# Efficient attention and mixture of depths: ranks as accumulated VectorE columns, a 0/1 matmul for the search, one unit's transposes and product in one slot

## The chip, the core and the metric

One core of a Trainium2 chip runs the whole problem. The metric is device microseconds of one execution, as the median of several. Five engines with instruction streams of their own take part: TensorE (PE in the rows; its weight loads are PEld), VectorE (DVE), ScalarE (ACT), GpSimd (POOL) and SyncE (SP, which here only issues DMAs). Each works its own instructions off in the order in which they were written and waits on semaphores for the others.

## What is computed

```python
def _attn_ref(q, k, v):                       # (8, 8, 576, 64) each
    q_s = softmax(q, axis=-1); k_s = softmax(k, axis=2)
    kv = np.einsum('bhsd,bhse->bhde', k_s, v)
    return np.einsum('bhsd,bhde->bhse', q_s, kv)

def _moe_ref(x, w_gate, w1, w2, capacity):    # x (8, 576, 512), capacity 128
    scores = np.einsum('bsd,d->bs', x, w_gate)
    out = x.copy()
    for b in range(B):
        top_idx = np.argpartition(-scores[b], capacity)[:capacity]
        xe = x[b, top_idx]
        ye = np.maximum(xe @ w1, 0.0) @ w2
        g = 1.0 / (1.0 + np.exp(-scores[b, top_idx]))
        out[b, top_idx] = x[b, top_idx] + g[:, None] * ye
```

The attention's heads are laid side by side and become x. Per batch the 128 tokens of highest score go through an MLP of 512 x 1024 x 512 and are written back over their rows.

## The kernel before

A **unit** is four heads of one batch: 16 units, two to a batch. Its 576 tokens lie on 128 partitions in five columns r (R = 5), the last half filled. For a unit u, `k_exp` and `q_exp` take exponentials on ScalarE, `v_copy` lays v beside a column of ones on VectorE, `kv_mm` multiplies K and V into 64 x 65 blocks (40 matmul instructions in the trace, since each fp32 matmul stands there twice), and `kv_out` inverts the sums (`krec`) and copies the blocks into a block-diagonal `kv_diag` that also holds a column for the score. `q_t(u, i)` transposes four columns of one half of the heads on TensorE, and ScalarE evacuates them into `qT`; `q_t_last` does the fifth column of both halves, evacuated by VectorE. `x_mm(u, i)` multiplies qT with kv_diag, and `x_out(u, i)` divides by q's sums into `xs` on VectorE and takes the scores into `sr`; the rows of the output then go out from the SP queue.

Of a batch's scores, `score` sums the head shares, `score_row` lays them as a row on all partitions (five transposes on TensorE, evacuated by ScalarE), `compare` makes on VectorE the 0/1 planes `less` and `ties` of every token against every other, `count` adds them over the partitions with 16 matmuls against ones (`ones_b`) and gives the ranks as a row, and `pick` finds for each of the 128 places the token whose rank it is (two passes of 640 columns that sum a product), computes the gate g and has POOL gather the rows from the output in DRAM (`xr`). `turn` transposes the gathered rows, `mlp1` and `mlp2` are the two halves of the MLP in eight pieces each, and `finish` adds and scatters.

The order is written by hand. The loop over slots s = 0 .. 19 works on unit s, prepares units s + 1 and s + 2, and lays MLP pieces between: batch b has its scores ready in slot 2b + 1, is compared in 2b + 2, counted and picked in 2b + 3 behind the fourth MLP piece, and its MLP runs in slots 2b + 4 (`turn` and `mlp1`) and 2b + 5 (`mlp2`). In slot s, TensorE has kv_mm(s + 1) and q_t(s + 1, 0) ahead of x_mm(s, 0); k_exp, v_copy and q_exp of unit s + 2 follow the products. A slot with mlp1 is called even below, one with mlp2 odd. PSUM holds two banks `tp` (transposes, K-V, counts), two pairs `x` and two banks `mm`. Loads of q, k and v go round three buffers, two DMAs each, all from SP's queue: load(s + 5) in slot s.

Of the kernel before, what the change touches and what calls it, by code (L numbers as in the profile page):

```python
# [8 lines left out]
F32 = mybir.dt.float32  # L9
# [8 lines left out]
def kernel(  # L18
# [20 lines left out]
    nc = tc.nc  # L39
# [5 lines left out]
    RP = R * P  # L45
# [6 lines left out]
    NG = 4 * R  # L52
    LOW = 2.0 ** -30
    WARM = 20
    assert S == 64 * (R + N2) and D == 64 and DM == H * D and DM == 512 and H % 4 == 0
    assert 1 < capacity < S and KF == 8 and NQ == 2
    HALF = RP // 2
# [27 lines left out]
    def load(u, which):  # L85
        b, qd = units[u]
        for what in which:
# [3 lines left out]
            for n, rows in enumerate((R, N2)):  # L91
                nc.sync.dma_start(
# [7 lines left out]
    load(0, "kvq")  # L100
# [12 lines left out]
    for n in range(20):  # L113
        nc.tensor.matmul(out=w_ps[part(n % 2), :132], lhsT=ones_f[:, :64], rhs=ones_f, start=True, stop=True)
# [33 lines left out]
    for h in range(2):  # L148
        nc.vector.memset(side[part(h), h:h + 1], 1.0)
    qrec = const.tile([P, NU, NG], F32, name="qrec")  # L150
    krec = const.tile([P, NU, 2], F32, name="krec")

    col_minus_p = const.tile([P, P], F32, name="col_minus_p")
    nc.gpsimd.iota(col_minus_p, pattern=[[1, P]], base=0, channel_multiplier=-1,
                   allow_small_or_imprecise_dtypes=True)
    after = const.tile([P, P], F32, name="after")
    tok_row = const.tile([P, RP], F32, name="tok_row")
    nc.gpsimd.iota(tok_row.rearrange("p (r m n) -> p r m n", r=R, n=2), pattern=[[1, R], [9, 64], [R, 2]], base=0,  # L158
                   channel_multiplier=0, allow_small_or_imprecise_dtypes=True)
    slot_no = const.tile([P, n_sl], F32, name="slot_no")  # L160
    for n, (k0, _) in enumerate(slots):
        nc.gpsimd.iota(slot_no[:, n:n + 1], pattern=[[1, 1]], base=k0, channel_multiplier=1,
                       allow_small_or_imprecise_dtypes=True)

    def late_constants():
        nc.vector.tensor_scalar(after, col_minus_p, 0.0, None, op0=OP.is_gt)
# [59 lines left out]
    def q_t_last(u):  # L226
        qe = st.pop(("qe", u))
# [7 lines left out]
    def x_mm(u, i):  # L235

        qT = st["qT", u] if i == 0 else st.pop(("qT", u))
        x_ps = ps.tile([P, 2, 512], F32, tag="x", name="x", bufs=2)
        x = x_ps[:, :, :6 * C].rearrange("p n (g h c) -> p n g h c", g=3, h=2)
        for r in range(R):  # L240
            nc.tensor.matmul(out=x[:, r // 3, r % 3], lhsT=qT[:, i, r], rhs=kv_diag[u % 2][:, i],  # L241
                             start=True, stop=True)
        st["x", u] = x
# [3 lines left out]
    def x_out(u, i):  # L247
        b, qd = units[u]
        if qd == 0 and i == 0:
            xs[b] = xp.tile([P, R, NQ, 2, 2, D], F32, tag="xs", name="xs")  # L250
            sr[b] = md.tile([P, NQ, 2, R, 2], F32, tag="sr", name="sr")
        x = st.pop(("x", u))
        rec = qrec[:, u].rearrange("p (i r h) -> p i r h", i=2, r=R)[:, i]
# [338 lines left out]
```

## Time and profile before

| | |
|---|---|
| time, median of 3 runs | 294.73 us (293.66 to 295.18) |
| profiled execution, its own time | 297.34 us |
| its span, first to last instruction | 295.5 us |
| mean granted TensorE clock | 0.920 |
| busy share PE, PEld, DVE, ACT, POOL | 80%, 65%, 49%, 34%, 7% |
| instructions | 5206 |
| DMA | 46.69 MB, 158 GB/s in the mean |

A busy TensorE is not TensorE at full clock: 1.00 of granted clock is 2.4 GHz, and the other level is 1.2. A stretch in which it waits and one in which it runs at the lower level both have to be looked for in the rows. The engines off the chain that sets the end may idle for nothing.

### The profile page before, as it was taken

How to read it: one execution, taken by the hardware profiler on the slowest of the kernel's cores; microseconds unless marked ns; L12 is line 12 of the kernel's file. 1: busy time of each engine (PE TensorE's matmuls, PEld its weight loads, DVE VectorE, ACT ScalarE, POOL GpSimd, SP SyncE). 2: the span in 40 equal slices, each digit the busy share in tenths (PEclk: the TensorE clock that was granted, in tenths of full speed). 3: DMA queues.
4: the chain of work that ended last, by engine and by line, in shares of the span. 5: the costliest groups of instructions: out<-in, count | busy, mean ns of one | idle time of the engine just before them, and what ended most of it. 6: DMA issues, size and time to landing. Idle time of an engine off the chain costs nothing.

```text
span 295.5 us, 5206 instructions
## 1 busy us (share of the span) xinstructions
PE 237.3 (80%) x2021; PEld 191.7 (65%) x2021; DVE 143.9 (49%) x506; ACT 99.1 (34%) x178; POOL 22.1 (7%) x32
## 2 busy tenths in 40 slices
PE   6468748229997699949996799969996999799990
PEld 6368638129963698529963798549963995484840
DVE  7454495503864176613863167615753386640001
ACT  3574444303352154315351153425351311130100
POOL 8000000100001100020001100020001000210101
PEclk9997796957999799998999599989999899999997
DMA  6999999880589218551649119220221122101101
GB/s 194 359 357 367 383 382 382 251 291 2 165 295 284 111 63 258 167 191 38 198 153 296 66 40 284 81 68 5 80 81 38 38 80 80 58 15 38 38 7 39
DMA packets 39329, 46.69 MB, mean 158 GB/s; under 512 B 2945, under 2 KB 36737, under 8 KB 39297
## 3 DMA queue, kind: packets, MB, share of 16 engines
q1 hardware_dynamic: 37472, 41.95, 43.4%
q0 software_dynamic: 1280, 4.20, 4.1%
q8 instruction: 18, 0.29, 0.4%
q10 hardware_dynamic: 544, 0.13, 0.2%
q14 instruction: 15, 0.11, 0.1%
HBM read 34.73 MB, written 11.53 MB: 157 GB/s over the span
## 4 chain that ended last, share of the span: by engine, by line
PE 65%; DMA 18%; issue 7%; DVE 3%; POOL 2%; ACT 2%; SPq 1%; POOLq 0%; ACTq 0%
PE mm L360 20%; PE mm L370 15%; DMA xr<-out_dram,idx 11%; PE x L241 10%; PE tp L194 8%; PE tp L221 4%; PE tp L312 4%; DMA q<-in_q_dram 3%; PE mm L346 2%; DMA out_dram<-xs 2%; DMA k<-in_k_dram 2%; DVE junk_p L325 2%; POOL tok_row L158 1%; ACT rank L314 1%; PE tp L230 1%
## 5 line engine op out<-in xcount | busy, mean ns | idle before, releaser
L360 PE MATMUL mm<-xT,w 128*128 128x128 f32 x512 | 65.2, 284 | 1.4 <-ACT xT L348 1.4
L360 PEld LDWEIGHTS mm<-xT,w 128*128 128x128 f32 x512 | 61.8, 199 | 2.5 <-ACT xT L348 1.9
L370 PE MATMUL mm<-w,hT 128*128 128x512 f32 x128 | 61.4, 600 | 0.0
L241 PE MATMUL x<-kv_diag,qT 128*128 128x132 f32 x320 | 43.3, 285 | 0.0
L241 PEld LDWEIGHTS x<-kv_diag,qT 128*128 128x128 f32 x320 | 41.3, 200 | 2.4 <-issue 2.4
L194 PE MATMUL tp<-v_ones,ke 128*64 128x65 f32 x640 | 29.6, 265 | 8.0 <-DVE v_ones L184 4.3
L194 PEld LDWEIGHTS tp<-v_ones,ke 128*64 128x64 f32 x640 | 27.1, 177 | 11.3 <-ACT qe L180 4.8
L257 DVE TENSOR_TENSOR xs<-x,qrec 128x384 f32<-128x384 f32 x64 | 31.4, 491 | 2.2
L370 PEld LDWEIGHTS mm<-w,hT 128*128 128x128 f32 x128 | 21.7, 191 | 14.9 <-issue 14.3
L223 ACT ACTIVATE qT<-tp,krec 128x512 f32<-128x512 f32 x32 | 22.0, 687 | 27.1 <-PE tp L221 27.0
L346 PE MATMUL mm<-ident,xr 128*128 128x128 f32 x32 | 7.2, 367 | 27.2 <-DMA xr<-out_dram,idx 27.2
L203 DVE RECIPROCAL krec<-tp 128x2 f32<-128x2 f32 x16 | 2.7, 170 | 48.7 <-PE tp L194 48.7
L256 DVE RECIPROCAL qrec<-x 128x6 f32<-128x6 f32 x64 | 11.8, 184 | 29.8 <-PE x L241 29.5
L346 PEld LDWEIGHTS mm<-ident,xr 128*128 128x128 f32 x32 | 4.7, 180 | 32.9 <-DMA xr<-out_dram,idx 32.4
L221 PE MATMUL tp<-ident,qe 128*128 128x128 f32 x128 | 21.6, 296 | 4.5 <-DVE krec L203 3.1
L330 POOL DMA_INDIRECT xr<-out_dram,idx x8 | 7.9, 988 | 219.9 <-PE tp L281 105.4
L180 ACT ACTIVATE qe<-q 128x640 f32<-128x640 f32 x32 | 21.7, 726 | 3.6 <-DMA q<-in_q_dram 3.6
L363 ACT ACTIVATE hT<-mm 128x512 f32<-128x512 f32 x16 | 9.6, 597 | 37.8 <-PE mm L360 37.8
L221 PEld LDWEIGHTS tp<-ident,qe 128*128 128x128 f32 x128 | 16.7, 154 | 7.9 <-issue 4.9
L173 ACT ACTIVATE ke<-k 128x1280 f32<-128x1280 f32 x16 | 20.2, 1261 | 2.8 <-DMA k<-in_k_dram 2.8
L378 DVE SCALAR_TENSOR_TENSOR o<-mm,g,xr 128x512 f32<-128x512 f32 x8 | 6.0, 749 | 27.1 <-PE mm L370 27.1
L348 ACT COPY xT<-mm 128x512 f32<-128x512 f32 x8 | 4.7, 586 | 42.2 <-PE mm L346 42.2
(71 smaller groups left out, 220.3 us busy)
## 6 DMA issues: line engine op xcount, KB each, us to landing
k<-in_k_dram SPq DMA_DIRECT2D x16, 320.0 KB, 5.0
v<-in_v_dram SPq DMA_DIRECT2D x16, 320.0 KB, 5.2
q<-in_q_dram SPq DMA_DIRECT2D x16, 320.0 KB, 5.7
out_dram<-xs SPq DMA_DIRECT2D x16, 320.0 KB, 2.8
k<-in_k_dram SPq DMA_DIRECT2D x16, 256.0 KB, 4.9
v<-in_v_dram SPq DMA_DIRECT2D x16, 256.0 KB, 5.5
q<-in_q_dram SPq DMA_DIRECT2D x16, 256.0 KB, 6.2
out_dram<-xs SPq DMA_DIRECT2D x16, 256.0 KB, 3.0
```

The source lines that it names most:

```text
L173: nc.scalar.activation(out=ke, in_=raw["k"][u % LD], func=AF.Exp)
L180: nc.scalar.activation(out=qe[:, i], in_=qr[:, i], func=AF.Exp)
L194: nc.tensor.matmul(out=kv[part(h), i], lhsT=ke[:, 2 * i + h, r], rhs=vo[:, 2 * i + h, r], start=(r == 0), stop=(r == N2))
L221: nc.tensor.transpose(out=t_ps[:, r * P:(r + 1) * P], in_=qe[:, i, r].rearrange("p h d -> p (h d)"), identity=ident)
L223: nc.scalar.activation(out=st["qT", u][:, i, :N2].rearrange("p r c -> p (r c)"), in_=t_ps, func=AF.Copy, scale=krec[:, u, i:i + 1])
L241: nc.tensor.matmul(out=x[:, r // 3, r % 3], lhsT=qT[:, i, r], rhs=kv_diag[u % 2][:, i], start=True, stop=True)
L256: nc.vector.reciprocal(out=rec[:, rows], in_=o[:, :, :, D])
L257: nc.vector.tensor_mul(xs[b][:, rows, qd, i], o[:, :, :, :D], rec[:, rows].to_broadcast([P, rows.stop - rows.start, 2, D]))
L312: nc.tensor.matmul(out=r_ps[:, a:z], lhsT=ones_b[:, :P], rhs=rhs, start=(n == 0), stop=(n == len(todo) - 1), skip_group_check=True)
L346: nc.tensor.transpose(out=t_ps[:, d * m:(d + 1) * m], in_=xr[:m, d * P:(d + 1) * P], identity=ident[:m, :m])
L360: nc.tensor.matmul(out=h_ps[:, f % 4 * m:(f % 4 + 1) * m], lhsT=w1[:, d, f * P:(f + 1) * P], rhs=xT[:, d, :m], start=(d == 0), stop=(d == ...
L370: nc.tensor.matmul(out=st["y", b, n][:m], lhsT=st["hT", b, n][:, f, :m], rhs=w2[:, f], start=(f == 0), stop=(f == KF - 1))
```

## The change

*Ranks.* Instead of 0/1 planes counted by matmuls, `compare(b, r)` is one VectorE pass over 576 columns (score row minus own score, against a threshold of a tiny number or zero that orders equal scores) with an accumulator that leaves the rank of each token in column r. *Search.* `pick` compares ranks with the place numbers into a 0/1 tile `hit` (one VectorE instruction of 640 columns) and multiplies it with `vals`, which holds token number and score split into five bf16 columns; five matmuls of 5 columns give both at once. POOL makes the score's three parts in `score`, five small operations per batch. The gate's exponential has moved into `gate`, later in the slot. *Products.* `x_out` has one reciprocal and one narrow product for both groups. *Order.* A unit's transposes now stand at the head of its own slot and its product behind them; kv_mm(s + 1) follows its own slot's first product; `v_copy(s + 1)`, `k_exp(s + 1)` and `q_exp(s + 1)` stand in slot s. `pick` stands near the slot's head. *Loads.* load(s + 4) in slot s, w1 and w2 earlier, unit 0's k from two queues. *Constants.* `late_constants` holds five 576-wide passes and a dozen small operations. The program's check of its ranges has six values instead of four.

```diff
     def late_constants():
-        nc.vector.tensor_scalar(after, col_minus_p, 0.0, None, op0=OP.is_gt)
+        nc.vector.tensor_single_scalar(odd_p, odd_p, 1, op=OP.bitwise_and)
...
+        nc.vector.tensor_copy(out=vals[:, :, :, 0], in_=whole.rearrange("p (b r) -> p b r", b=B))
...
+        for r in range(R):
+            nc.vector.tensor_scalar(not_before[:, r], order_minus_p, float(r * P), TINY, op0=OP.is_ge, op1=OP.mult)
...
+        nc.vector.reciprocal(out=rec, in_=x[:, :, :, D])
         for n, rows in enumerate((slice(0, 3), slice(3, R))):
...
-            nc.vector.reciprocal(out=rec[:, rows], in_=o[:, :, :, D])
...
-            nc.vector.tensor_mul(sr[b][:, qd, i, rows], o[:, :, :, D + 1], rec[:, rows])
...
-    def compare(b):
-        s, srow = st["s", b], st["srow", b]
...
-    def count(b):
...
+    def compare(b, r):
...
+        nc.vector.scalar_tensor_tensor(junk, st["srow", b], st["s", b][:, r:r + 1], not_before[:, r],
+                                       op0=OP.subtract, op1=OP.is_ge, accum_out=st["rank", b][:, r:r + 1])
...
+            nc.vector.tensor_tensor(out=hit[:, :, :m], in0=slot_no[:, None, k0:k0 + m].to_broadcast([P, R, m]),
+                                    in1=rank.to_broadcast([P, R, m]), op=OP.is_equal)
+            c_ps = bank("tp", 2)
             for r in range(R):
...
+                nc.tensor.matmul(out=c_ps[:m, :NV], lhsT=hit[:, r, :m], rhs=vals[:, b, r],
+                                 start=(r == 0), stop=(r == N2))
...
+            if here:
+                q_t(s, 0)
+                q_t_last(s)
             if first:
                 each(turn, mlp_b)
-            if s + 1 < NU:
+            else:
+                pieces(1)
+            if here:
+                q_t(s, 1)
+            if chosen is not None:
+                pick(chosen)
+            if not first:
+                pieces(1)
+            if here:
+                x_mm(s, 0)
+                x_out(s, 0)
+            if after:
+                k_exp(s + 1)
+                v_copy(s + 1)
+            pieces(2 if first else 1)
+            if last:
+                x_mm(s, 1)
+                x_out(s, 1)
+                x_store(s)
+                score(ends)
+            if after:
                 kv_mm(s + 1)
                 kv_out(s + 1)
...
+            if compared is not None:
+                for r in range(2):
+                    compare(compared, r)
+            pieces(1)
+            if here and not last:
                 x_mm(s, 1)
                 x_out(s, 1)
...
+                x_store(s)
             if last:
                 score_row(ends)
-                compare(ends)
+                for r in range(R):
+                    compare(ends, r)
+            if chosen is not None:
+                each(gate, chosen)
+            if ends is not None and not last:
+                score(ends)
+            if after:
+                q_exp(s + 1)
...
+            if compared is not None:
+                for r in range(2, R):
+                    compare(compared, r)
             pieces(2)
```

TensorE in slot 4, the first with an MLP, before: L346 turns the gathered rows, L194 is K-V, L360 mlp1 (four matmuls a piece), L221 and L230 are q's transposes, L241 its product.

```order
L346 MATMUL mm<-ident,xr 128x128 x4
L194 MATMUL tp<-v_ones_183,ke 64x65 x20
L360 MATMUL mm<-xT,w_162 128x128 x4
L221 MATMUL tp<-ident,qe 128x128 x4
L241 MATMUL x<-kv_diag_181,qT 128x132 x5
L221 MATMUL tp<-ident,qe 128x128 x4
L360 MATMUL mm<-xT,w_162 128x128 x4
L241 MATMUL x<-kv_diag_181,qT 128x132 x5
L360 MATMUL mm<-xT,w_162 128x128 x4
L230 MATMUL tp<-ident,qe 128x128 x2
L360 MATMUL mm<-xT,w_162 128x128 x20
```

The same slot now; L397 turns the gathered rows, L260 and L269 are q's transposes, L280 the product, L411 mlp1, L233 K-V:

```order
L260 MATMUL tp<-ident,qe 128x128 x4
L269 MATMUL tp<-ident,qe 128x128 x2
L397 MATMUL mm<-ident,xr 128x128 x4
L260 MATMUL tp<-ident,qe 128x128 x4
L280 MATMUL x_189<-kv_diag_178,qT 128x132 x5
L411 MATMUL mm<-xT,w_159 128x128 x8
L233 MATMUL tp<-v_ones_180,ke 64x65 x20
L411 MATMUL mm<-xT,w_159 128x128 x4
L280 MATMUL x_191<-kv_diag_178,qT 128x132 x5
L411 MATMUL mm<-xT,w_159 128x128 x20
```

K-V has gone from the slot's head to behind the first product and two pieces, and the transposes, now the unit's own, to the head.

VectorE in slot 5, before, where the first MLP's batch is in mlp2 and batch 1 is searched: L184 lays v beside the ones, L232 evacuates the last transposes, L325 is the search.

```order
L184 COPY v_ones_183<-v_84 128x20x64
L232 TENSOR_TENSOR qT<-tp,krec 128x2x128
L325 SCALAR_TENSOR_TENSOR junk_p,sel<-rank,slot_no,tok_row 128x640
L325 SCALAR_TENSOR_TENSOR junk_p,sel<-rank,slot_no,srow 128x640
L328 TENSOR_SCALAR idx<-sel 128x1
L335 TENSOR_SCALAR g<-g 128x1
L336 RECIPROCAL g<-g 128x1
```

The same slot now, from its head; L364 to L374 are the search, L292 to L298 x_out, L223 v_copy:

```order
L271 TENSOR_TENSOR qT<-tp,krec 128x2x128
L364 TENSOR_TENSOR hit<-slot_no,rank 128x640
L372 TENSOR_REDUCE no<-tp 128x1
L373 TENSOR_SCALAR idx<-no 128x1
L374 TENSOR_REDUCE no<-tp 128x1
L292 RECIPROCAL qrec<-x_189 128x12
L295 TENSOR_TENSOR xs<-x_189,qrec 128x3x128
L295 TENSOR_TENSOR xs<-x_189,qrec 128x2x128
L298 TENSOR_TENSOR sr<-x_189,qrec 128x12
L223 COPY v_ones_175<-v_82 128x20x64
```

v's copy stands now behind the search and the first x_out of the slot that uses it, and before behind the products of the slot ahead of that.

VectorE from v_copy(0) on at the start, before; L203 to L211 are kv_out, L232 evacuates unit 0's last transposes, L184 is the copy of v:

```order
L184 COPY v_ones_178<-v_82 128x20x64
L166 TENSOR_SCALAR after<-col_minus_p 128x128
L203 RECIPROCAL krec<-tp 128x2
L208 TENSOR_TENSOR prod<-tp,wg 128x128
L210 TENSOR_REDUCE kvw<-prod 128x2
L211 TENSOR_TENSOR kv_diag_181<-kvw,side 128x4
L232 TENSOR_TENSOR qT<-tp,krec 128x2x128
L184 COPY v_ones_183<-v_83 128x20x64
```

Now, from inside the constants, which follow kv_out(0), to the same point:

```order
L202 COPY valid_r<-beyond 128x1
L203 TENSOR_SCALAR valid_r<-valid 128x1
L205 TENSOR_SCALAR not_before<-order_minus_p 128x576 x5
L271 TENSOR_TENSOR qT<-tp,krec 128x2x128
L292 RECIPROCAL qrec<-x_189 128x12
L295 TENSOR_TENSOR xs<-x_189,qrec 128x3x128
L295 TENSOR_TENSOR xs<-x_189,qrec 128x2x128
L298 TENSOR_TENSOR sr<-x_189,qrec 128x12
L223 COPY v_ones_180<-v_83 128x20x64
```

Before, one small constant stands ahead of kv_out(0); now the constants stand between kv_out(0) and the evacuation of the transposes.

## Rows read from the trace of the kernel before

**Rows 1.** Table of stretches: bounds, length, busy us (and instructions) PE, PEld, DVE, ACT, POOL, clock, DMA share, GB/s

```profile
15.09:22.70 7.61, 4.95 (x71) 4.61 (x71) 4.58 (x18) 5.61 (x9) 0.00 (x0) 1.00 1.08 357
...
40.94:64.60 23.66, 9.73 (x91) 8.63 (x92) 11.62 (x42) 5.90 (x12) 1.13 (x1) 0.76 0.98 335
64.60:98.31 33.71, 29.50 (x246) 23.89 (x246) 17.07 (x60) 12.21 (x22) 0.95 (x1) 0.91 0.58 185
...
131.11:164.22 33.11, 28.35 (x245) 22.91 (x245) 17.07 (x60) 12.21 (x22) 1.97 (x2) 0.93 0.50 160
...
227.76:254.83 27.07, 25.61 (x195) 20.32 (x196) 16.97 (x64) 5.38 (x12) 1.96 (x2) 0.94 0.19 64
254.83:273.05 18.22, 16.99 (x103) 12.28 (x104) 5.13 (x19) 2.83 (x6) 1.96 (x2) 1.00 0.10 31
273.05:295.50 22.45, 14.71 (x84) 10.30 (x82) 1.50 (x2) 1.78 (x3) 1.97 (x2) 0.93 0.08 27
```

**Rows 2.** List of waits: who waited for whom: us in total, times, longest

```profile
PE mm L346 <- DMA xr<-out_dram,idx: 27.2, 7, 8.7
```

**Rows 3.** Chain that ended last, one pair of slots: start us, us, what

```profile
131.77 2.18 PE tp L194 x40
133.95 1.79 PE mm L360 x8
...
137.74 0.89 PE mm L360 x8
...
145.33 1.32 PE tp L194 x40
...
147.71 0.44 PE tp L221 x4
148.14 1.13 PE x L241 x10
...
152.77 0.86 PE mm L370 x2
153.63 0.83 PE tp L312 x8
...
154.96 0.98 PE tp L312 x8
...
159.09 5.09 DMA xr<-out_dram,idx
```

**Rows 4.** TensorE in order of time near 164 and 255: start, us, what, [idle before, releaser]

```profile
164.22 1.11 PE L346 MATMUL mm<-ident,xr 128*128 128x128 f32 x4 [4.24 <-DMA xr<-out_dram,idx]
...
254.83 0.66 PE L346 MATMUL mm<-ident,xr 128*128 128x128 f32 x4 [1.39 <-DMA xr<-out_dram,idx]
...
256.16 3.84 PE L360 MATMUL mm<-xT,w 128*128 128x128 f32 x32 [0.68 <-ACT xT L348]
```

**Rows 5.** Groups by line and shape: line, engine, operation, names, shapes, count | busy us, mean ns | idle before

```profile
L223 ACT ACTIVATE qT<-tp,krec 128x512 f32<-128x512 f32 x32 | 22.0, 687 | 27.1 <-PE tp L221 27.0
...
L180 ACT ACTIVATE qe<-q 128x640 f32<-128x640 f32 x32 | 21.7, 726 | 3.6 <-DMA q<-in_q_dram 3.6
...
L257 DVE TENSOR_TENSOR xs<-x,qrec 128x384 f32<-128x384 f32 x32 | 17.8, 558 | 1.1
...
L257 DVE TENSOR_TENSOR xs<-x,qrec 128x256 f32<-128x256 f32 x32 | 13.6, 425 | 1.1
L184 DVE COPY v_ones<-v 128x1280 f32<-128x1280 f32 x16 | 13.1, 820 | 1.9 <-DMA v<-in_v_dram 1.9
...
L206 ACT COPY kv_diag<-tp 64x130 f32<-64x130 f32 x32 | 8.4, 262 | 26.9 <-DVE krec L203 26.5
...
L325 DVE SCALAR_TENSOR_TENSOR junk_p<-rank,slot_no,tok_row 128x640 bf16<-128x640 f32 x8 | 7.1, 885 | 18.3 <-ACT rank L314 18.3
...
L256 DVE RECIPROCAL qrec<-x 128x6 f32<-128x6 f32 x32 | 6.3, 196 | 29.8 <-PE x L241 29.5
...
L292 DVE TENSOR_SCALAR less<-srow,s 128x640 bf16<-128x640 f32 x8 | 4.4, 546 | 0.0
```

More of the change, by code (lines that the diff above doesn't have):

```diff
@@ L112 @@
     w_ps = bank("tp", 2)
-    for n in range(20):
-        nc.tensor.matmul(out=w_ps[part(n % 2), :132], lhsT=ones_f[:, :64], rhs=ones_f, start=True, stop=True)
+    w_ps2 = bank("tp", 2)
+    for n in range(24):
+        a, c = ((0, 0), (1, 1), (0, 1), (1, 0))[n % 4 if n >= 12 else n % 2]
+        nc.tensor.matmul(out=(w_ps, w_ps2)[a][part(c), :66], lhsT=ones_f[part(a), :64],
+                         rhs=ones_f[part(a), :66], start=True, stop=True)
     for n in range(WARM):
@@ L158 @@
[L158 to L163, printed above, removed]
[L165 to L166 removed]
+    x_buf = []
@@ L273, in score @@
         st["s", b] = s
+        left = md.tile([P, R], F32, tag="left", name="left")
+        for c in range(2, NV):
+            nc.gpsimd.tensor_copy(out=vals[:, b, :, c], in_=raw_s if c == 2 else left)
+            if c < NV - 1:
+                nc.gpsimd.tensor_sub(left, raw_s if c == 2 else left, vals[:, b, :, c])
     def score_row(b):
@@ L431, in general @@
                     x_out(u, i)
-            score(b)
+                x_store(u)
+            score(b, 0)
             score_row(b)
-            compare(b)
-            count(b)
+            for r in range(R):
+                compare_exact(b, r)
             pick(b)
+            each(gate, b)
             each(turn, b)
@@ L459, in sums_in_range @@
         return number
-    def prepare(u):
-        k_exp(u)
-        v_copy(u)
-        q_exp(u)
     LAG = 4
@@ L503, in pieces @@
                     f_next += 1
-            ends = s // 2 if s % 2 == 1 and s < NU else None
-            compared = (s - 2) // 2 if s % 2 == 0 and 2 <= s < NU else None
+            here = s < NU
+            after = s + 1 < NU
+            last = s == NU - 1
+            ends = s // 2 if here and s % 2 == 1 else None
+            compared = s // 2 - 1 if s % 2 == 0 and 2 <= s < NU else None
             chosen = (s - 3) // 2 if s % 2 == 1 and 3 <= s < NU else None
@@ L514 @@
+            if after:
[8 more added lines that the diff above has]
+            if after:
                 kv_mm(s + 1)
                 kv_out(s + 1)
-                pieces(1)
-                q_t(s + 1, 0)
-            elif not last:
-                pieces(1)
-            if s < NU:
-                x_mm(s, 0)
-                x_out(s, 0)
@@ L535 @@
[L535 to L549 removed]
+                x_store(s)
             if last:
                 score_row(ends)
[L552 removed]
+                for r in range(R):
+                    compare(ends, r)
@@ L553 @@
             pieces(2)
-            if last:
-                pieces(1)
-            pieces(1)
             if ends is not None and not last:
                 score_row(ends)
-            pieces(1)
+            pieces(3 if first else 2)
             if busy and odd == 1:
```

247 lines of the change are left out of this document (130 added, 117 removed).

## Prediction, made before the changed kernel was run

> **What bounds the kernel now.** I read the table of stretches first [rows 1]. Cut at the transposes of the gathered rows (L346), which open the MLP of a batch, the program falls into a start (to 64.60 us), five pairs of slots (163.2 us to 227.76), two last stretches and a tail. In a pair such as 131.11 to 164.22 TensorE is busy for 28.35 of 33.11 us, VectorE for 17.07, ScalarE for 12.21, and DMA for half: TensorE bounds, and it is neither full nor at full clock (0.93). Where it loses time the chain shows [rows 3]. The gather runs 5.09 us from 159.09, and the transposes that start at 164.22 have 4.24 us of nothing ahead of them [rows 4]. After such a gap TensorE runs at the lower level: the 40 K-V matmuls take 2.18 us against 1.32 later in the pair, and the first eight MLP matmuls 1.79 against 0.89, so another 1.76 us. The list of waits says the same in sum: 27.2 us of TensorE's waiting for gathered rows, seven times, at most 8.7 [rows 2].
>
> What a pair costs at full clock comes from the pieces in [rows 3]: K-V 2 x 1.32, transposes of q 2 x (0.44 + 0.44 + 0.22), products 4 x 1.13, first MLP half 8 x 0.89, second 8 x 0.86, turning xr 0.44, score rows 0.55 (five transposes): 24.3 us. Gap 4.2, slow clock 1.8 and the count (153.63 to 155.94) 2.3 make 32.6 of the 33.1.
>
> **The change, part by part.** *The count leaves TensorE.* 16 ones-matmuls with their evacuations go: 2.3 us a pair [rows 3]. In their place are five 0/1 matmuls of 5 columns, whose like no row shows. Between nothing (they slip in beside weight loads) and 0.8 (half the count they replace) I take 0.3.
>
> *The gather is issued a slot earlier.* The search now stands near the head of slot 2b+3, and the MLP opens in 2b+4 as before. From search to opening lie some 11 us of slot against a gather of 5.09: the gap and the slow clock behind it go, 6.0 us a pair.
>
> *VectorE.* The nine compares and five tie products of a batch become five 576-wide passes with an accumulator. A 640-wide one takes 0.89 [rows 5]; 576 columns with the reading of the accumulator I put at 0.88, so 4.4 in all; the two 640-wide searches become one 640-wide compare. From 0.56 at 384 and 0.43 at 256 columns that is 0.82. VectorE's sum falls and stays far from TensorE's; its order matters more.
>
> *What comes late next.* One unit's work is now in one line in one slot. kv_mm(s+1) stands behind v_copy(s+1), which stands on VectorE behind x_out(s,0), which waits for x_mm(s,0). Before, v_copy was done a slot ahead. x_out is a reciprocal, two products and a narrow product (priced as the reciprocal): 0.20 + 0.56 + 0.43 + 0.20 = 1.4; v_copy 0.82 [rows 5]; with 0.15 of hand-over 2.35 us. Between x_mm(s,0) and kv_mm(s+1) TensorE has two MLP pieces in the even slot (1.78), one in the odd (0.86). It stalls 0.6 and 1.5 us. Two smaller ones: in the even slot the second transposes need the first's PSUM bank, evacuated in 0.69 [rows 5] beside 0.66 of other work, 0.2 with hand-over; in the odd slot score_row waits for x_out(s,1) and three small score operations with two pieces (1.72) as cover, 0.4. Three of the compares end the even slot; VectorE then has the last q product (as before) and the 0/1 compare ahead of it. By durations that ends within 0.1 us of where TensorE asks for it, so nothing is taken, 0.8 if the cover is short.
>
> So a pair: 24.3 + 0.3 + 0.8 + 1.9 = **27.3 us**. If none of the stalls showed it would be 24.6; if each were 0.8 longer than worked out in both slots, 28.9. The first pair I give 1 us of slow clock. From the first opening to the sixth: before 64.60 to 227.76, 163.2 [rows 1]; after 5 x 27.3 + 1 = 137.5. **-25.7.**
>
> *The start.* The wait of 8.7 for the first gather goes, but the four slots without an MLP have no filler any more. In line a slot is: transposes 0.44, evacuation 0.8, second transposes 0.44, product 1.13, x_out 1.4, v_copy 0.82, K-V 1.32, reciprocal and two copies 0.8, first exp of q 0.73 [rows 3, 5]: 7.9 us, 0.3 of hand-over, and 3.3 us of it on a TensorE at 0.76 as in [rows 1] (+1.0): 9.2. Before, kv_mm(1) to kv_mm(4) is 15.09 to 40.94, 8.6 a slot. Ahead of kv_mm(1) now stand the new constants (five 576-wide passes of at most 0.55 and a dozen small ones of at most 0.20 [rows 5], 5.1 us at most; 4.2 taken, since they overlap at their ends; all on VectorE in front of slot 0's q product) and that slot's product in line, 2 us: 21.3. Three slots bring 27.6, the score row of slot 1 with its wait 2.4, five compares and the 0/1 compare ahead of slot 3's q product 5.2: kv_mm(4) at 56.5. To the first opening come 1.3 + 1.13 + 1.4 + 0.6 + 0.55 + 0.7 + 0.66 and 1 of clock: 7.3, so 63.8 against 64.6. **-0.8**, between -6 (constants and half the compares beside DMA waits) and +5 (half clock throughout). The loads cover this: each is issued three slots ahead as before. The weights move up the SP queue, w1 to just behind unit 3 and w2 behind units 5 and 6; at the 335 GB/s of [rows 1], unit 5 is there by about 45 and is wanted after 60. x_store now stands on SP ahead of the next loads, as before.
>
> *The end.* From the sixth opening to the eighth, before 227.76 to 273.05, 45.3 [rows 1]. After: rest of slot 14 12.2, slot 15 11.1 of work and 1.0 for the last score row. In slot 16 five compares, the gate and finish stand on VectorE ahead of the last 0/1 compare, and the search is ahead of the MLP pieces on TensorE: after score_row come its evacuation 0.9, the compares 4.4, gate and finish 1.1, the 0/1 compare 0.82, 7.3 with hand-over, covered by four second-half pieces and the turn of xr, 3.9: a stall of 3.4. With 0.44 + 0.3 + 7.1 that is 11.2, slot 17 6.9, slow clock after the stall 1.0: 43.4. **-1.9** (0 to -4). The last 22.45 us keep their chain, 0.
>
> Sum: -0.8 - 25.7 - 1.9 = -28.4. The profiled execution took 297.34 us around a span of 295.5 and would take 268.9; it lay 2.6 above the median of 294.73, and against that the forecast is **266.3 us**.
>
> **Rivals.** *The clock does not stay up.* The new stalls come twice a slot. If one in each of the 11 slots that prepare another unit costs what the gaps of [rows 3] cost, 1.76 us, the time is 266.3 + 19.4 = 286. Against it: at 254.83 TensorE had just been idle 1.39 us and was idle another 0.68 before its 32 MLP matmuls, which took 3.84 us against 3.6 elsewhere, and that stretch has a granted clock of 1.00 [rows 1, 4]. For it: the longest new stall, 1.5, is longer than any of these. The Trainium skill, "TensorE: Matmul & The Clock Gate", section "A second HAM failure mode: psum-queue depth-cycling", speaks against the change here: frequent small idles between groups of matmuls make the clock fall and recover over and over. By that rule this rival's 286 would hold; the 1.00 of [rows 1] does not bear it out at 1.39 us. Chance 14%.
>
> *The stalls are covered and the start is short.* VectorE takes the next instruction a little before the one ahead is out, so x_out and v_copy may take 0.4 less; with pairs of 25.6 (-8.5) and a start of 60 (-4) the time is 254. Chance 16%.
>
> *Slower.* One place: the MLP slots run at the clock of the slots before them, 0.76 [rows 1], because transposes, product and copies of one unit hang in one line there too. A pair is then 24.6 / 0.76 + 2.7 = 35.1; five are +39 and slots 14 and 15 +8 on the forecast, 313 us. It decides against the change from a clock under 24.6 / (32.6 - 2.7) = 0.82 on. Against it: half of TensorE's work in these slots is MLP, which waits for nothing in the line. Chance 4%.
>
> *The gather is not what holds the opening*, and the pair keeps its 33 us because the evacuation of the gathered rows or VectorE's finish comes last. Against it: in [rows 2] the opening waits for the gather and nothing else. Time 294. Chance 1%.
>
> **How the numbers follow.** Forecast 65%, clock 14%, better cover 16%, slower 4%, no effect 1%. The forecast's own bounds are 266.3 - 10 and + 12 (start ±5, five pairs +8 or -8, end ±2, not all at once). The range of 254 to 281 leaves out the clock rival's upper half, the slower case and the lower tail of the better one, about 2 in 10. Faster by over 0.5% (what a measurement of this kernel can tell from no change): 0.94; within 0.5%: 0.02; slower: 0.04.
>
> **What would show it.** Right: no wait of TensorE for gathered rows; pairs of about 27 us with a granted clock over 0.97; waits of kv_mm for v_copy near 1.5 and 0.6 us; the first opening near 64; one stall of some 3 us in slot 16 for the 0/1 compare. Wrong: K-V matmuls of 2 us and more inside the pairs (clock), openings before 60 or after 69 (the start), a 576-wide pass well off 0.88, or a wait of TensorE for the 0/1 compare in each odd slot.

## The result and the profile after

| | before | changed kernel |
|---|---|---|
| time, median | 294.96 us (293.66 to 299.37, 4 runs) | 278.71 us (276.59 to 279.93, 4 runs) |
| ratio | | 0.946 (95% interval 0.938 to 0.953) |
| profiled execution, span | 295.5 us | 277.0 us |
| first opening (turn of xr) | 64.60 | 70.24 |
| first to sixth opening, five pairs | 163.16 | 139.61 |
| sixth to eighth opening | 45.3 | 44.64 |
| behind the eighth | 22.45 | 22.51 |

The forecast was 266.3 us in a range of 254 to 281. The kernel became faster, less than forecast: the pairs gave 23.6 of the 25.7 us that they were to give, and the start grew by 5.6 us where it was to shrink by 0.8.

The table of stretches of the changed kernel answers to [rows 1]: bounds in us, length, then busy us and instructions of PE, PEld, DVE, ACT and POOL, granted clock, DMA share, GB/s.

```profile
0.00:22.07 22.07, 10.91 (x121) 9.72 (x121) 10.23 (x48) 7.17 (x10) 3.37 (x18) 1.00 0.90 285
22.07:30.43 8.36, 5.44 (x70) 4.73 (x71) 4.29 (x14) 4.42 (x7) 0.00 (x0) 1.00 0.98 324
30.43:45.49 15.06, 9.88 (x76) 8.68 (x76) 5.00 (x17) 5.12 (x9) 0.98 (x5) 0.63 1.02 340
45.49:60.80 15.31, 9.47 (x76) 8.55 (x76) 9.36 (x28) 4.42 (x7) 1.17 (x1) 0.61 0.63 203
60.80:70.24 9.44, 6.71 (x61) 6.18 (x62) 2.77 (x13) 2.68 (x7) 0.98 (x5) 0.68 0.72 234
70.24:98.54 28.30, 26.28 (x236) 20.86 (x236) 15.02 (x48) 11.31 (x20) 2.01 (x6) 0.97 0.57 181
...
126.36:154.19 27.83, 25.63 (x236) 20.25 (x235) 15.22 (x49) 11.22 (x20) 3.01 (x7) 1.00 0.60 188
...
209.85:234.94 25.09, 23.35 (x190) 18.39 (x189) 15.50 (x48) 8.19 (x15) 2.97 (x7) 1.00 0.21 70
234.94:254.49 19.55, 16.76 (x92) 12.51 (x90) 6.48 (x27) 1.98 (x4) 2.33 (x2) 0.91 0.08 28
```

Two things stand out. A pair has gone from 33.11 to 27.83 us at a granted clock of 1.00 instead of 0.93. And three stretches of the start run at 0.61 to 0.68, lower than the 0.76 of before: more of the time at the 1.2 GHz level, where 1.00 is 2.4 GHz throughout.

The list of TensorE's waits (who for whom: us in total, times, longest) answers to [rows 2]:

```profile
PE tp L233 <- DVE v_ones L223: 17.3, 15, 2.2
PE tp L331 <- DVE s L316: 7.2, 8, 2.2
PE tp L368 <- DVE hit L364: 6.0, 2, 3.2
```

No wait for gathered rows is left in it, where before there were 27.2 us. First among TensorE's is now K-V waiting for the copy of v (L223): the line that the change made. The kernel before had this wait in two places only, 4.3 us in sum.

TensorE in order of time, in one pair (start, us, what, idle before it and releaser):

```profile
154.98 0.66 PE L260 MATMUL tp<-ident,qe 128*128 128x128 f32 x4 [0.18 <-ACT qT L262]
...
158.91 1.39 PE L233 MATMUL tp<-v_ones,ke 128*64 128x65 f32 x40 [0.37 <-DVE v_ones L223]
...
167.47 1.02 PE L421 MATMUL mm<-w,hT 128*128 128x512 f32 x2
168.33 0.60 PE L260 MATMUL tp<-ident,qe 128*128 128x128 f32 x4
168.89 0.28 PE L368 MATMUL tp<-vals,hit 128*128 128x5 bf16 x5
...
171.09 1.02 PE L421 MATMUL mm<-w,hT 128*128 128x512 f32 x2
173.41 1.39 PE L233 MATMUL tp<-v_ones,ke 128*64 128x65 f32 x40 [1.30 <-DVE v_ones L223]
...
179.05 0.76 PE L331 MATMUL tp<-ident,s 128*128 128x128 f32 x5 [0.36 <-DVE s L316]
```

These are the four stalls of the forecast, each in its place: 0.18, 0.37, 1.30 and 0.36 us against 0.2, 0.6, 1.5 and 0.4. K-V behind the 1.30 us of waiting runs its 40 matmuls in 1.39 us, at full clock.

The start of the same view, from the first K-V on:

```profile
10.64 2.43 PE L233 MATMUL tp<-v_ones,ke 128*64 128x65 f32 x40 [4.58 <-DVE p_int L142]
...
22.07 1.39 PE L233 MATMUL tp<-v_ones,ke 128*64 128x65 f32 x40 [2.15 <-DVE v_ones L223]
...
30.43 2.08 PE L233 MATMUL tp<-v_ones,ke 128*64 128x65 f32 x40 [2.15 <-DVE v_ones L223]
32.44 2.28 PE L280 MATMUL x<-kv_diag,qT 128*128 128x132 f32 x10
...
45.49 2.44 PE L233 MATMUL tp<-v_ones,ke 128*64 128x65 f32 x40 [2.15 <-DVE v_ones L223]
...
55.94 0.30 PE L368 MATMUL tp<-vals,hit 128*128 128x5 bf16 x5 [3.17 <-DVE hit L364]
```

In every slot without an MLP, TensorE stands idle 2.15 us for v ahead of K-V. From the second such slot on K-V takes 2.08 to 2.44 us instead of 1.39, and the product behind it 2.3 to 2.6 instead of 1.39. The loads do not hold these slots: in the list of waits only the k and the v of unit 0 are waited for, once each.

### The profile page after: what moved, and what is told of

It reads as the page before. It is cut to its first block, busy times and chain, and to the rows that moved or that the text cites. A ratio compares the mean times of both kernels' runs of the same rounds, so it can differ in the third digit from the quotient of the medians.

```text
span 277.0 us, 4988 instructions
## 1 busy us (share of the span) xinstructions
PE 226.2 (82%) x1933; PEld 181.1 (65%) x1933; DVE 131.1 (47%) x435; ACT 92.0 (33%) x162; POOL 27.8 (10%) x74
## 4 chain that ended last, share of the span: by engine, by line
PE 56%; DVE 21%; DMA 9%; issue 5%; ACT 4%; SPq 3%; POOL 0%; POOLq 0%; ACTq 0%; DVEq 0%
PE mm L411 14%; PE mm L421 12%; PE x L280 12%; PE tp L233 9%; DMA v<-in_v_dram 7%; DVE xs L295 6%; PE tp L260 5%; DVE junk L344 4%; DVE v_ones L223 4%; SPq L96 2%; DMA q<-in_q_dram 2%; DVE qrec L292 2%; PE tp L331 2%; ACT qT L262 2%; SPq L303 1%
## 5 line engine op out<-in xcount | busy, mean ns | idle before, releaser
L411 PE MATMUL mm<-xT,w 128*128 128x128 f32 x512 | 62.8, 281 | 0.7 <-ACT xT L399 0.7
L411 PEld LDWEIGHTS mm<-xT,w 128*128 128x128 f32 x512 | 60.4, 196 | 1.4 <-ACT xT L399 1.0
L280 PEld LDWEIGHTS x<-kv_diag,qT 128*128 128x128 f32 x320 | 45.5, 216 | 6.2 <-issue 5.7
L280 PE MATMUL x<-kv_diag,qT 128*128 128x132 f32 x320 | 48.1, 304 | 0.0
L233 PE MATMUL tp<-v_ones,ke 128*64 128x65 f32 x640 | 26.0, 244 | 21.9 <-DVE v_ones L223 17.3
L233 PEld LDWEIGHTS tp<-v_ones,ke 128*64 128x64 f32 x640 | 24.1, 157 | 28.1 <-issue 28.1
L344 DVE SCALAR_TENSOR_TENSOR junk<-srow,s,not_before 128x576 bf16<-128x576 f32 x40 | 32.6, 816 | 2.4 <-ACT srow L336 1.5
L245 ACT COPY kv_diag<-tp 64x130 f32<-64x130 f32 x32 | 8.4, 262 | 66.8 <-DVE krec L242 66.4
L295 DVE TENSOR_TENSOR xs<-x,qrec 128x384 f32<-128x384 f32 x64 | 28.5, 486 | 1.1
L260 PE MATMUL tp<-ident,qe 128*128 128x128 f32 x128 | 23.0, 309 | 5.7 <-ACT qT L262 2.7
L260 PEld LDWEIGHTS tp<-ident,qe 128*128 128x128 f32 x128 | 16.5, 158 | 15.5 <-ACT qT L262 8.9
L292 DVE RECIPROCAL qrec<-x 128x12 f32<-128x12 f32 x32 | 7.4, 232 | 35.1 <-PE x L280 33.4
L223 DVE COPY v_ones<-v 128x1280 f32<-128x1280 f32 x16 | 13.1, 818 | 6.2 <-DMA v<-in_v_dram 6.2
```

The source lines that it names most:

```text
L223: nc.vector.tensor_copy(out=v_ones[u % 2][:, :, :, :D], in_=raw["v"][u % LD])
L233: nc.tensor.matmul(out=kv[part(h), i], lhsT=ke[:, 2 * i + h, r], rhs=vo[:, 2 * i + h, r], start=(r == 0), stop=(r == N2))
L260: nc.tensor.transpose(out=t_ps[:, r * P:(r + 1) * P], in_=qe[:, i, r].rearrange("p h d -> p (h d)"), identity=ident)
L280: nc.tensor.matmul(out=x[:, r // 3, g:g + 2], lhsT=qT[:, i, r], rhs=kv_diag[u % 2][:, i], start=True, stop=True)
L292: nc.vector.reciprocal(out=rec, in_=x[:, :, :, D])
L295: nc.vector.tensor_mul(xs[b][:, rows, qd, i], x[:, n, :g, :D].rearrange("p (r h) d -> p r h d", h=2), rec[:, n, :g].rearrange("p (r h) -> ...
```

## Experiments

Each kernel was timed beside the kernel before; a ratio is to that. The openings are where the turn of xr begins, as in the table above.

### The search put back to its late place

```diff
-            if chosen is not None:
+            if chosen is not None and not here:
                 pick(chosen)
...
+            if chosen is not None and here:
+                pick(chosen)
+                each(gate, chosen)
             pieces(2)
             if ends is not None and not last:
                 score_row(ends)
```

> The changed kernel with its search (0/1 compare, matmuls, gather, gate) moved back to where the kernel before had it, behind the fourth MLP piece of the odd slot. If the gap behind the gather is what the early search took away (4.2 us of nothing and 1.8 us of low clock a pair), pairs go from 27.8 to about 33.8 us and the time from 278.7 to 309 to 316. If the gather is not what holds the MLP's opening, pairs stay at 27.8 and the time stays within 1% of 278.7.

Measured: 304.32 us, ratio 1.030 (1.024 to 1.036); opening at 71.52, pairs 31.1 to 33.2, a little under what I expected (33.8, and 309 us or more). So 25.6 us are lost and all of the change's gain with them. But not by the gather alone:

```profile
PE tp L368 <- POOL left L323: 16.1, 6, 2.7
PE tp L368 <- DVE hit L364: 6.9, 2, 5.7
PE mm L397 <- DMA xr<-out_dram,idx: 6.6, 4, 3.5
```

The wait for gathered rows is 6.6 us; the larger part is the new search itself, whose matmuls (L368), late in the slot, meet GpSimd's making of the next batch's score parts and VectorE's compare in line. The place of the search decides, as expected, but this kernel alone does not say by which wait.

### The kernel before with the early search alone

```diff
                 pieces(1)
+                if chosen is not None:
+                    count(chosen)
+                    pick(chosen)
                 q_t(s + 1, 0)
...
-            if chosen is not None:
+            if chosen is not None and s + 1 >= NU:
                 count(chosen)
                 pick(chosen)
```

> The kernel before, with its count and its search moved behind the first MLP piece of the odd slot; planes, ones-matmuls and the order of the units stay. If the place of the search is worth the whole gain and the one-line order of the units costs something, pairs go from 32.6 to about 27, the opening of the first MLP comes before 60 us, and the time falls to 257 to 265, under the changed kernel's 278.7. If the ranks on VectorE or the one-line order carry the gain, the time stays above 279.

Measured: 258.87 us (258.26 to 258.94), ratio 0.876 (0.872 to 0.881). One step of the change, an edit of four lines, is worth some 36 us of the kernel before, more than the whole change. TensorE's wait for gathered rows falls from 27.2 us to 2.8. Openings at 55.15 and 189.31. Its table of stretches for the five pairs between, and of the second pair its two ends and the count (98.66 to 100.30) in order of time:

```profile
55.15:189.31 134.16, 134.16 (x1225) 109.21 (x1226) 83.58 (x299) 59.93 (x110) 8.83 (x9) 0.98 0.58 184
```

```profile
83.85 0.60 PE L346 MATMUL mm<-ident,xr 128*128 128x128 f32 x4
...
98.66 0.30 PE L312 MATMUL tp<-less,ones_b 128*128 128x320 bf16 x1
...
100.30 0.60 PE L221 MATMUL tp<-ident,qe 128*128 128x128 f32 x4
...
110.22 0.60 PE L346 MATMUL mm<-ident,xr 128*128 128x128 f32 x4
```

TensorE is busy for the whole 134.16 us, nothing waited for: 28.70 in the first pair, whose first matmuls run at the lower level, and 26.37 in each of the four behind it. Against the changed kernel it is 15.1 us earlier at the first opening and 1.46 shorter in a pair, though it still makes the count, from 98.66 to 100.30. Of the change it has the early search alone, so the rest of the change, as it is laid there, costs 20 us together.

### Filling TensorE in the start

```diff
+            if s < LAG:
+                f_ps = bank("mm", 2)
+                for n in range(18):
+                    nc.tensor.matmul(out=f_ps[:, :P], lhsT=ones_b[:, :P], rhs=ones_b[:, :P], start=True, stop=True)
             pieces(2 if first else 1)
```

> The changed kernel with 18 extra bf16 matmuls of 128 columns, 1.2 us at full clock, in the wait ahead of K-V in each of the slots 0 to 3; their result is used by nothing. If the low clock (K-V at 2.4 against 1.4 us, products at 2.3 against 1.1) is what made the start 6 us longer than predicted, K-V and products come down to 1.4 and 1.1 there, the first MLP opens near 65 instead of 70.2, and the time falls by 4 to 6 us. If VectorE and ScalarE alone set the pace of these slots, the opening stays at 70 or goes up by up to 4 us.

Measured: 273.89 us, ratio 0.927 (0.922 to 0.933), opening at 65.69, 4.55 earlier than in the changed kernel; the pairs are as they were. K-V in the same two slots, in order of time:

```profile
29.51 1.39 PE L233 MATMUL tp<-v_ones,ke 128*64 128x65 f32 x40 [1.14 <-DVE v_ones L223]
43.22 1.39 PE L233 MATMUL tp<-v_ones,ke 128*64 128x65 f32 x40 [0.58 <-DVE v_ones L223]
```

More work on TensorE, and less time: 1.39 us instead of 2.08 and 2.44. The dummies fill time in which K-V waited for v anyway, and what comes back is the clock: the three stretches at 0.63, 0.61 and 0.68 in the changed kernel are at 0.75, 0.88 and 0.81 here, as the table of stretches has them:

```profile
29.51:43.22 13.71, 9.86 (x94) 8.77 (x94) 4.90 (x17) 5.12 (x9) 1.00 (x5) 0.75 1.06 362
43.22:57.48 14.26, 8.30 (x94) 7.30 (x94) 9.35 (x28) 4.42 (x7) 1.17 (x1) 0.88 0.68 218
57.48:65.69 8.21, 5.34 (x62) 4.71 (x63) 2.67 (x13) 2.68 (x7) 0.99 (x5) 0.81 0.89 293
```

### The constants spread, and unit 0 through one queue

```diff
-        late_constants()
...
+            if s == 0:
+                late_ints()
+            if s == 1:
+                late_valid()
+                late_order(0, 3)
+            if s == 2:
+                late_order(3, R)
```

> The changed kernel with its constants taken out of the stretch between kv_out(0) and slot 0's q product and laid behind v_copy in slots 0, 1 and 2, where VectorE waits for K-V. The prediction put 4.2 us for them on the path to the first opening: by that the opening goes from 70.2 to 66 or 67 and the time falls by 3 to 4 us. If slot 0's transposes and product, at low clock beside them, took that long anyway, the opening and the time stay within 1 us.

Measured: 278.42 us, ratio 0.938 (0.933 to 0.943), opening at 69.97: 0.3 us. The constants, which I had put at 4.2 us in line, cost nothing that shows. In the changed kernel VectorE has them from 14.63 to 18.11, beside transposes and a product that run at the lower level at that time; of that product, which begins at 17.50, only the fifth column, its last, needs what VectorE does behind them.

```diff
-    load(0, "k", (nc.sync, nc.scalar))
-    load(0, "vq")
+    load(0, "kvq")
```

> The changed kernel with unit 0's k, v and q issued by SyncE alone, in the order of the kernel before. v(0) was there at 9.67 us against 8.62 before. If the split over two queues put half of v ahead of k and made v late, K-V of unit 0 starts about 1 us earlier and so does the first opening, and the time falls by about 1 us. If not, both stay.

Measured: 277.14 us, ratio 0.935 (0.931 to 0.940), opening at 68.71, 1.5 earlier. With k split over two queues the first copy of v begins at 9.67, against 8.62 before and 8.58 here. The K-V of unit 0 begins at 9.55 here and at 9.82 to 10.64 in the kernels with two queues.

### Both middle pieces of an odd slot ahead of K-V

```diff
-            if not first:
+            if not first and not after:
                 pieces(1)
...
-            pieces(2 if first else 1)
+            pieces(2 if first or after else 1)
```

> The changed kernel with both middle MLP pieces of the odd slots between the product and K-V, instead of one ahead of the product and one behind. If K-V waits there because one piece covers 0.86 of the 2.2 us that x_out and v_copy take, its wait of 1.30 us comes down to about 0.44, pairs from 27.8 to 27.0, and the time falls by 4 to 5 us. If the wait only moves (to x_mm for its transposes, or to score_row), pairs stay at 27.8.

Measured: 274.12 us, ratio 0.925 (0.919 to 0.931); pairs of 26.97, 0.86 shorter, and K-V's wait there down from 1.30 to 0.43. The wait for v is on the path at its full length.

### v's copy a slot ahead

```diff
-                v_copy(s + 1)
+                if s == 0:
+                    v_copy(1)
...
+            if s + 2 < NU:
+                v_copy(s + 2)
             if after:
                 q_exp(s + 1)
```

> The changed kernel with v's copy alone moved a slot ahead: v_copy(s+2) behind the second output of slot s (and behind the scores of an odd slot) instead of v_copy(s+1) behind the first output; everything else of the one-line order stays. Theory (the pair's stalls are v's copy standing in the line x_out, v_copy, kv_mm): K-V no longer waits in either slot, 1.30 + 0.37 us less a pair and some 0.3 around them, pairs 25.8 to 26.2, and 0.8 to 1.2 us less in each of slots 1 to 3 of the start, opening 67 to 68.5, 266 to 269 us. Rival (the line of one unit's transposes, product and copies holds the slot by other steps, and the copy that now stands ahead of the compares or the 0/1 compare makes TensorE wait there): pairs 27 or more with a wait for hit near 1 us in each odd slot, 273 to 279 us.

Measured: 265.75 us (263.48 to 269.06), ratio 0.898 (0.888 to 0.908). One instruction per slot, moved, takes 13 us off the changed kernel. That this is about the time I expected is luck: two misses cancel. The opening is at 61.94, 8.3 us earlier, which is far more than I expected; the pairs are 26.99, longer than I expected, but for one of 26.27. The stretches that answer to slot 3 and to a pair:

```profile
40.67:54.07 13.40, 7.57 (x77) 6.54 (x76) 9.35 (x28) 4.42 (x7) 1.17 (x1) 0.75 0.88 294
...
169.51:196.50 26.99, 25.49 (x237) 20.20 (x236) 15.13 (x49) 11.23 (x20) 3.66 (x7) 1.00 0.39 125
```

And TensorE in order of time in two pairs:

```profile
130.68 0.28 PE L368 MATMUL tp<-vals,hit 128*128 128x5 bf16 x5
...
133.84 1.39 PE L233 MATMUL tp<-v_ones,ke 128*64 128x65 f32 x40
...
157.69 0.27 PE L368 MATMUL tp<-vals,hit 128*128 128x5 bf16 x5 [0.87 <-ACT qT L262]
...
160.83 1.39 PE L233 MATMUL tp<-v_ones,ke 128*64 128x65 f32 x40
```

VectorE's 0/1 compare in the same two pairs:

```profile
129.81 0.82 DVE L364 TENSOR_TENSOR hit<-slot_no,rank 128x640 bf16<-128x640 f32 x1
...
156.07 0.81 DVE L364 TENSOR_TENSOR hit<-slot_no,rank 128x640 bf16<-128x640 f32 x1
```

In the pairs K-V waits for nothing, so the copy was the line's dear step. In the start K-V of unit 1, whose copy has not moved, still waits 2.15 us; that of unit 2 waits 0.81, for k's exponentials, and the two behind it for nothing. Half of what that gives in a pair is lost again at the 0/1 matmul: 0.87 us of waiting in four places, where the one pair without it is 0.72 shorter. The rival had foretold a wait of that size there, by a late compare, but that is not it: the compare is out at 130.63 and at 156.88, in both cases 0.1 us behind the transposes ahead of the matmul, and only the second time does TensorE stand on until ScalarE has evacuated those transposes. Why it goes by that event there stays open.

### Three mends together

The edits of the fill, of the two pieces and of the one queue in one kernel.

> The changed kernel with three edits together: the 18 dummy matmuls ahead of K-V in slots 0 to 3, both middle pieces of an odd slot between the product and K-V, and unit 0 loaded through one queue. Theory (the three losses lie in different places: clock and load in the start, the wait for v in the pairs): they add, 278.7 - 4.8 - 4.6 - 1.5, about 268 us (266 to 270), opening 64 to 65, pairs 27.0. Rival (clock and load of the start are one loss): opening 65.7 as with the dummies alone, 270 to 271; and if the pairs' gain hung on the state of the start, 273 or more.

Measured: 268.18 us, ratio 0.909 (0.888 to 0.930); opening at 64.21, pairs of 26.97. The three single gains are 4.8, 4.6 and 1.6 us, 11.0 in sum; together they give 10.5. So they lie in different places.

### The new ranks alone, and with the early search in the old unit order

The kernel before with new ranks, 0/1 matmul and constants (and the change's `x_out`, its six checks and unit 0's two queues); search and unit order stay:

```diff
-            nc.vector.tensor_scalar(less[:, r, :end], srow[:, :end], own, None, op0=OP.is_lt)
...
+        nc.vector.scalar_tensor_tensor(junk, st["srow", b], st["s", b][:, r:r + 1], not_before[:, r],
+                                       op0=OP.subtract, op1=OP.is_ge, accum_out=st["rank", b][:, r:r + 1])
```

> The kernel before with the new ranks, the 0/1 matmul and the constants alone; the search stays where the kernel before has it and a unit's pieces keep their order. Theory (the ranks save TensorE some 2 us a pair and shorten the chain from the last rank to the gather by 1 to 1.5 us, and each is worth its full length as long as the gathered rows are waited for): 275 to 285 us, the wait for xr at an odd opening 5 to 7 us instead of 7 to 8.7. Rival (with the search late the new one waits on VectorE's hit and on GpSimd's values in line, which takes the gain back): 290 to 297 us, with waits for hit of 1 us or more in each slot.

Measured: 283.32 us, ratio 0.951 (0.921 to 0.981). Its waits:

```profile
PE mm L401 <- DMA xr<-out_dram,idx: 17.4, 5, 6.3
PE tp L372 <- POOL left L327: 12.7, 6, 3.5
```

Both theories hold in part: the wait for gathered rows falls from 27.2 to 17.4 us, and the new search waits in line for GpSimd's parts instead.

Then the same kernel with the search moved early, at three places of the odd slot. First behind the slot's first piece:

> New ranks, new search and its early place, but the units in the order of the kernel before: transposes and v's copy a slot ahead of the product; the constants spread over slots 0 and 1. If the one-line order is a pure loss (1.3, 0.4, 0.4 and 0.2 us of waits a pair and a start without filler), pairs come to 25 to 26 us, the first opening to 55 to 60 and the time to 248 to 256. If the one-line order is needed for the early search to pay, it stays above 275.

Measured: 257.77 us, ratio 0.873 (0.868 to 0.877), pairs of 26.49, more than I expected and no better than the early search alone, since TensorE waits for the 0/1 compare, up to 5.3 us in one place. Then behind the second transposes and a piece:

```diff
-                if chosen is not None:
-                    pick(chosen)
                 q_t(s + 1, 0)
...
+            if chosen is not None and s < NU:
+                pick(chosen)
             if s < NU:
                 x_mm(s, 1)
```

> As e6_hybrid, with the search one product and one piece later in the odd slot, since TensorE there waited up to 5.3 us for the 0/1 compare, which stood on VectorE behind five compares, v's copy and q's last product. If that wait is what kept e6_hybrid's pairs at 26.5 us, they come to 25 to 25.5, the time from 257.8 to 250 to 253, and the gather still lands ahead of the opening. If the gather then comes late, a wait of 1 to 3 us for gathered rows shows and the time stays at 256 to 260.

Measured: 258.21 us, ratio 0.872 (0.868 to 0.876), pairs of 25.87 with some 0.8 us of waiting for the 0/1 compare, and an end of 46.1. That is 5 us and more above what I expected, by the end and by what is left of the wait. Then later by one product, with the last search at the end of slot 16, the check of the ranges a slot later and unit 0 through one queue:

```diff
             if s < NU:
                 x_mm(s, 1)
+            if chosen is not None and s < NU:
+                pick(chosen)
+            if s < NU:
                 x_out(s, 1)
```

> The new ranks and search in the unit order of before, with the search of an odd slot one piece later than in e7_hybrid_search_mid (behind the product of the second half, ahead of the first output transposes), the last pick at the end of slot 16 and unit 0 loaded through one queue. Theory (what is left of the wait for hit, some 0.8 us a pair and several us in slot 16, is a search laid too early for VectorE): pairs 25.1 to 25.4, first opening about 56, sixth to eighth opening 42 instead of 46.1, 248 us (245 to 252). Rival (the later search makes the gathered rows late or the wait moves to v and the scores): pairs 25.9 or more, 255 to 259 us.

Measured: **251.70 us** (251.11 to 254.79), ratio 0.854 (0.834 to 0.874). Its table of stretches, and the search in order of time:

```profile
133.05:157.98 24.93, 24.93 (x236) 20.46 (x234) 15.32 (x48) 11.19 (x20) 3.65 (x7) 1.00 0.67 211
```

```profile
151.85 0.27 PE L371 MATMUL tp<-vals,hit 128*128 128x5 bf16 x5
151.98 1.10 PE L424 MATMUL mm<-w,hT 128*128 128x512 f32 x2
```

A pair is 24.93 us with TensorE busy throughout. From the five 0/1 matmuls to the next instruction are 0.13 us, where the count took 1.64; the difference, 1.5, answers to the 1.44 by which the pair is shorter than with the early search alone. So beside the early search, which left TensorE full, the new ranks bring their gain only where their own search waits for nothing. The place was a matter of one product. Opening at 55.56, sixth to eighth 42.58; what still shows there is the wait of the last sum for `good` (the check of the ranges), 3.28 us at 225.38, in the end.

## Why the prediction was right or wrong

The forecast moved the span from 295.5 to 267.1; it came to 277.0. The 9.9 us between are 6.4 in the start, 2.1 in the pairs, 1.2 in the end and 0.1 behind it. The medians lie 12.4 apart, since the forecast took off 2.6 us by which the profiled execution of before lay above its median, and the profiled one of after lay on its own (278.86). The time is in the stated range, but 0.4 us beyond the forecast's own upper bound of 266.3 + 12, in the part that the range kept for the clock rival. The sign of being wrong for the start, an opening after 69, came true; of the signs of being right all but the opening near 64 did, the clock with 0.97 in the first pair just at its mark.

**The gather: right.** No wait for xr is left, and the early search alone, in the old order, takes the wait from 27.2 us to 2.8 and makes the pair 26.37 by itself. From [rows 3] I had 24.3 + 2.3 for work and count there, 26.6.

**The pair: right, 27.83 against 27.3.** The work is 24.93 (the pair in which nothing waits) against 24.3 + 0.3. The stalls are 2.21 against 2.7. The 0.69 left over, which I had not counted, is the rest of the busy time of TensorE, 25.63 against 24.94, and nearly all of it lies ahead of the stalls. The two mlp2 matmuls at 167.47 take 1.02 us, but the next group begins 0.86 behind their start. Where nothing follows at once, as ahead of the wait at 173.41, these last 0.16 us are time of their own, and so ahead of each of the four stalls: 0.64 in all. A stall there costs its wait and 0.16. The durations on which the stalls rest came out as estimated:

```profile
L344 DVE SCALAR_TENSOR_TENSOR junk<-srow,s,not_before 128x576 bf16<-128x576 f32 x40 | 32.6, 816 | 2.4 <-ACT srow L336 1.5
...
L364 DVE TENSOR_TENSOR hit<-slot_no,rank 128x640 bf16<-128x640 f32 x8 | 6.5, 815 | 0.0
L344 DVE DVE_READ_ACCUMULATOR junk<-srow,s,not_before 128x1 f32 x40 | 3.3, 83 | 0.0
```

In this list by line and shape (count, busy us, mean ns) the 576-wide pass and the reading of its accumulator take 0.82 and 0.08; I had 0.88 for both. The 0/1 compare takes 0.82, as worked out. The 0/1 matmuls, for which I took 0.3, take 0.13 in the fastest kernel.

**The clock in the pairs: the rival fell.** Idle times of up to 1.30 us, four a pair, leave the granted clock at 1.00 in four of the five pairs and at 0.97 in the first. By the rule of the Trainium skill ("TensorE: Matmul & The Clock Gate", section "A second HAM failure mode: psum-queue depth-cycling"), which has frequent small idles bring the clock down, these pairs would be the 286 us of that rival; the trace does not bear it out there. In the start the clock does fall, to 0.61 to 0.68, but among idles of 2 us and more, which are not small ones. The slower rival, MLP slots at the clock of the slots before them, fell by the same rows.

**The start: the step that failed, 70.24 against 63.8.** The term that failed is TensorE's clock in the slots without an MLP. I had seen the line (product, x_out, v_copy, K-V) and counted its steps, and then took TensorE's clock from the start of before, 0.76, which is 1.0 us a slot. The line itself, with its wait in each slot, brings the clock further down. In slots 2 and 3 TensorE is busy for 9.88 and 9.47 us where slot 1, at full clock, has 5.44 and the score row and the 0/1 matmuls add 0.7 and 0.3: 3.7 us a slot where I had 1.0. Slot 1 came at 8.36 against 9.2; the slots 2 and 3 miss by +3.5 and +0.9 (the compares of slot 3 I had over-priced: TensorE waits 3.17 us for the 0/1 compare, against 5.2), and the way to the first opening by +2.1. How the level falls on single slots differs between executions, their sum hardly: with the two pieces moved, an edit that touches none of these slots, K-V of unit 1 begins at 21.22 instead of 22.07, and the opening is at 70.20. Filling TensorE brings 4.55 us back, the load through one queue 1.5: 6.1 of the 6.4, and 6.0 with both in one kernel (opening at 64.21). In the other direction, the 4.2 us for the constants were wrong too (0.3 measured), so that kv_mm(1) came at 22.07, near my 21.3, is luck: the K-V of unit 0 was a microsecond later, by the load, and it, the first transposes and the product ran at the lower level. One cause of that level may be a part of the change that I had not priced: the matmuls on constants with which the program opens were cut and end at 6.06 us instead of 7.68. TensorE is then idle 4.58 us ahead of that K-V instead of 1.91, and it takes 2.43 us instead of 1.39. In every run with the shorter opening it takes 2.27 to 2.44, with one queue too; in the kernel before and that with the early search alone it takes 1.39. No run puts the matmuls back by themselves, so this cause is not shown. Against before the start is 5.6 us longer, just outside the upper bound of +5 that I had given it.

**What hung on v's copy.** Taking it out of the line gives 8.3 us in the start, not the 0.8 a slot of its own length: with it go most of the wait of 2.15 us in three of the four slots and much of the low clock (slot 3 at 0.75 instead of 0.61, TensorE busy 7.57 instead of 9.47). My sum had the copy's length in the line, and 1.0 us a slot for the clock; that its place costs twice, by the whole wait and by the clock that follows, was missing.

**The end: 44.64 against 43.4.** Of the 1.2 us, 0.8 lie in slots 14 and 15 (25.09 against 24.3), where I had left out the stalls of 0.18 and 0.37 us. Slot 16's stall is 2.79 us against 3.4; the slow clock behind it is larger than the 1.0 I gave: the 64 first-half matmuls take 9.02 us there and 7.41 in the fastest kernel.

**What I had not asked.** I costed the change as a whole and never its parts alone. The early search needs neither the new ranks nor the new order of a unit. Alone it gives some 36 us; the ranks add 7 beside it at the right place. The changed kernel is 27 us behind that one (278.71 against 251.70): v's copy moved alone gives 13 of them and one queue 1.6; the rest is what else is different, the unit in one line and the places of the searches above all, which no run separates.

## What to carry to other kernels

When the profile shows a transfer waited for at the same place in each round, try first to issue it a slot earlier and change nothing else. Keep what an in-order engine needs next (here the copy of v) a slot ahead of it: in line it is paid as a wait, and in slots where nothing else fills that wait again in the clock behind it. Cheaper work on the bounding engine showed its full gain here only once nothing waited there, and its place had to be right to one product.

## What was not expected of the hardware

The granted clock of the first stretch reads 1.00 (0.00 to 22.07 in the table of the changed kernel), yet the K-V matmuls at 10.64 took 2.43 us for 40, against 1.39 at 22.07. In the kernel before, whose first stretch reads 1.00 too, the same group took 1.39 at 9.59. In the first microseconds the duration of a known group tells the level, and the clock column doesn't.

TensorE stood idle 2.15 us before the rows of K-V at 22.07 and at 30.43, and K-V took 1.39 us after the first and 2.08 after the second. With the search put back to its late place, which changes nothing up to there, it is the other way round:

```profile
21.07 2.44 PE L233 MATMUL tp<-v_ones,ke 128*64 128x65 f32 x40 [2.15 <-DVE v_ones L223]
...
31.57 1.39 PE L233 MATMUL tp<-v_ones,ke 128*64 128x65 f32 x40 [2.15 <-DVE v_ones L223]
```

One wait of this length did not set the level, and the same code gave either level at the same place; what set it I can't tell from these runs.

In the two kernels with the new search late, its matmuls wait for GpSimd (12.7 and 16.1 us in six waits), which at that moment makes the parts of the next batch, in other columns of the same tile `vals`. That the wait goes by the tile and not by the columns is argued from this, not tried.
